# Soft-MoE tail of a fused attention kernel: last weight blocks loaded by column halves, first half combined and stored between

## The chip, the cores and the metric

One core of one Trainium2 chip runs the whole program. The metric is device microseconds of one execution. Before the change three runs gave a median of 540.23 us (538.64 to 541.44).

## The reference, cut to what matters

First an attention over 8 batches, 8 heads, 576 tokens and 64 dimensions: scores scaled by 1/8, everything more than `tau` under the row's maximum dropped, softmax, product with V. Its output, 4608 tokens by 512 columns, is the input `x` of a soft mixture of experts with 8 experts of 4 slots each:

```python
logits = x @ phi                                   # 4608 x 32
d = softmax over the tokens;  slot_input = d.T @ x # 32 x 512
for e in range(8):
    slot_out[e] = relu(slot_input[e] @ w1[e]) @ w2[e]   # w1 512x1024, w2 1024x512, 16.8 MB + 16.8 MB
c = softmax over the slots (of the same logits)
out = c @ slot_out                                 # 4608 x 512, 9.4 MB
```

All numbers are float32 in memory. Nothing of `out` can be written before `slot_out` is there, and each column of `slot_out` needs that column of all rows of all of `w2`.

## The kernel before

The attention takes the first 470 us or so. It is scheduled by a planner with a table of due times, and the change does not touch it. The program after it ("the tail") is in the order in which it is written.

**Weights.** `w1` and `w2` are cut into 64 blocks of 128 partitions by 1024 numbers (512 KB, 4 KB in each partition, which are 4 KB in a row in memory too). Blocks 1 to 32 are `w1`, 33 to 64 `w2`; a `w2` block holds 256 rows of one expert, two rows in each partition (`j`). `load_unit` (line 487) takes the next block and issues one DMA on SyncE's queue. 45 blocks are loaded during the attention; the other 19 are issued as the first product frees their places.

**Products.** Experts are worked on in two groups of four (`a`), each expert in its own 32 columns of TensorE's array, so that four matmuls run side by side. `stage1` (line 1051) multiplies by `w1`, `relu` and `hidden` make the transposed hidden layer `hz`, and `stage2` (line 1084) multiplies by `w2` in steps `k` of four blocks (one per expert). Of the last group, k = 0 and 1 end in the PSUM tile `so`; k = 2 goes by halves of 256 columns into two tiles `end[0]` and `end[1]`; k = 3 (the last four blocks) is spread over 128-column quarters, each in its own 32 columns of the array (lines 1088 to 1094).

**Slots.** `slots` (line 1123) adds the partial sums of the groups with a matmul by the constant `st4`, once on the part that is in `so` and once on the rest. ScalarE then writes `sh`, VectorE subtracts its own rounding from half the rows (lines 1135 and 1137), and `sh` (float32r) is ready in halves of columns.

**Output.** `combine` (line 1127) runs over 18 jobs of 256 tokens: 16 of 512 of a batch's 576 tokens (`b`, `k`), then two of the 64 left tokens of each batch. Each job is two matmuls of a transposed coefficient tile (`cTs[b]`) with `sh`, a copy by ScalarE, a copy by VectorE, and a DMA of 512 KB on SyncE's queue, 4 KB in a row per partition. The jobs of left rows are stored by two DMAs each, 64 partitions and 2 KB in a row. `ct` (line 1020) makes a coefficient tile: GpSimd multiplies, TensorE transposes (line 1045), ScalarE casts (line 1046), VectorE subtracts (line 1047); two are made early, the others one after each pair of jobs. The stores wait on SyncE's queue behind the loads and are issued in the order written.

Of the kernel before, what the change touches and what calls it, by code (L numbers as in the profile page):

```python
# [10 lines left out]
F32 = mybir.dt.float32  # L11
F32R = mybir.dt.float32r
AF = mybir.ActivationFunctionType
ALU = mybir.AluOpType
# [8 lines left out]
    k=2, q=2, vv=2, r=3, ri=1, nmx=4, thr=4, p2=4, pL=1, pTa=1, pTb=1, pla=1, plb=1, plL=1,  # L23
# [13 lines left out]
WARM = 17  # L37
FILL = 14
NHOST = 19
TABLE = {}  # L40
for _n, _v in (
    ("batch", [
# [321 lines left out]
def softmax_attention_soft_moe(  # L364
# [17 lines left out]
    nc = tc.nc  # L382
    B, HP, D, _, S = qT.shape
    NP = B * HP
    N9 = 9
    DM = out.shape[1]
    E, _, F = w1.shape
    NS = phi.shape[1]
    SPE = NS // E
    SM = 512  # L390
# [14 lines left out]
        out=st1, in_=ident.rearrange("p (g s) -> p s g", g=4), axis=AX.X, op=ALU.add  # L405
# [5 lines left out]
    def few(n):  # L411
# [12 lines left out]
        out=flag8, in0=tau_sb, scalar1=0.0, scalar2=0.125, op0=ALU.is_ge, op1=ALU.mult  # L424
# [22 lines left out]
    with tc.tile_pool(name="ps_up", bufs=1, space=PSUM) as up:  # L447
        t = up.tile([128, 512], F32, name="up")
# [5 lines left out]
        k=([128, S], F32), q=([128, 2, S], F32), vv=([128, 640], F32), p2=([128, 2 * S], F32), pL=([128, S + 3 * SL], F32),  # L454
        pTa=([128, 2, 4, QA], F32), pTb=([128, 2, 4, S - QA], F32), pla=([128, QA], F32), plb=([128, SM - QA], F32),
        ss=([128, S], F32), xT=([128, S], F32), x=([128, 4, DM], F32), xl=([128, DM], F32),
        d=([128, 384], F32), R=([128, S], F32), rt=([128, 128], F32),
# [17 lines left out]
    NG = E // 4  # L475
# [9 lines left out]
    where = {}  # L485

    def load_unit(t):

        if len(where) == len(units):
            return  # L490
        i, kind, _, e, k = units[len(where)]
        where[i] = t
        if kind == 0:
            nc.sync.dma_start(t, w1[e, k * 128:(k + 1) * 128, :])
        else:
            nc.sync.dma_start(t, w2[e, k * 256:(k + 1) * 256, :].rearrange("(p j) f -> p (j f)", j=2))


    rows = [slice(0, 64), slice(64, 128)]
# [497 lines left out]
    def ttile(name):  # L997
        return ps_t.tile([128, 512], F32, tag="t", name=name)
# [21 lines left out]
    def ct():  # L1020


        if len(cTs) == len(blocks):
            return
        while len(c4s) < min(len(cTs) + 2, len(blocks)):
            c4s.append(c_block(*blocks[len(c4s)]))
        k = blocks[len(cTs)][1]
        c4 = c4s[len(cTs)]
        n = 128 * k
        t = tx.tile([128, SM], F32R, tag="cT", name=f"cT{len(cTs)}", bufs=3)  # L1030
        if len(cTs) < 2:
            w = two(f"ct{len(cTs)}", "h00" if cTs else "h01")
            for i in range(k):
                split(w, i, c4[:, i].rearrange("p g s -> p (g s)"))
            tv = t.rearrange("p (i g q) -> p i g q", i=4, g=2)
            for g in range(2):
                wv = w[g][:, 0:256].rearrange("p (i q) -> p i q", i=4)
                nc.scalar.copy(tv[:, :, g], wv)
                nc.vector.tensor_tensor(
                    out=tv[64:128, :, g], in0=wv[64:128], in1=tv[64:128, :, g].bitcast(F32), op=ALU.subtract)  # L1040
            cTs.append(t)
            return
        w = ttile(f"ct{len(cTs)}")
        for i in range(k):
            tr(w[:, i * 128:(i + 1) * 128], c4[:, i].rearrange("p g s -> p (g s)"))
        nc.scalar.copy(t[:, 0:n], w[:, 0:n])
        nc.vector.tensor_tensor(  # L1047
            out=t[64:128, 0:n], in0=w[64:128, 0:n], in1=t[64:128, 0:n].bitcast(F32), op=ALU.subtract)
        cTs.append(t)
# [22 lines left out]
    def hidden(a, hid):  # L1072
        for n in range(2):
# [3 lines left out]
            for g, m in enumerate(rows):  # L1077
# [3 lines left out]
                    op=ALU.mult,  # L1081
                )

    def stage2(a, k):
        t = [where[n_units // 2 + a * 16 + k * 4 + g].rearrange("p (j f) -> p j f", j=2) for g in range(4)]

        if a == NG - 1 and k == 3:
            for g in range(4):
                for j in range(2):
                    for c in range(4):  # L1090
                        nc.tensor.matmul(
                            end[c // 2][c * 32:(c + 1) * 32, c % 2 * 128:(c % 2 + 1) * 128],
                            hz[:, a, k * 2 + j, g * 32:(g + 1) * 32], t[g][:, j, c * 128:(c + 1) * 128],
                            start=False, stop=(g == 3 and j == 1), tile_position=(0, 32 * c), skip_group_check=True)
            return
        apart = a == NG - 1 and k == 2
        for q, dst in enumerate(end if apart else [so]):
            c = slice(q * DM // 2, (q + 1) * DM // 2) if apart else slice(0, DM)
            for j in range(2):
                for g in range(4):  # L1100
                    nc.tensor.matmul(
                        dst[g * 32:(g + 1) * 32, 0:c.stop - c.start], hz[:, a, k * 2 + j, g * 32:(g + 1) * 32],
                        t[g][:, j, c], start=(j == 0 and (apart or a == 0 and k == 0)),
                        stop=(j == 1 and not apart and a == NG - 1 and k == 1),
                        tile_position=(0, 32 * g), skip_group_check=True)
        for g in range(4):
            load_unit(where[n_units // 2 + a * 16 + k * 4 + g])

# [2 lines left out]
    def otile(name):  # L1111
        cnt[0] += 1
        k = cnt[0] % 6
        return ps_h.tile([128, 512], F32, tag=("h01", "h10", "h11")[k // 2], name=name) if k % 2 else ttile(name)
# [6 lines left out]
        return [t for i, t in sorted(last.values(), key=lambda x: x[0])]  # L1121

    def slots(w, x, q, first):
        nc.tensor.matmul(w[:, 0:DM // 2], st4.rearrange("p g s -> p (g s)"), x[:, q * DM // 2:(q + 1) * DM // 2],
                         start=first, stop=not first)

    def combine():

        cols = [slice(n * DM // 2, (n + 1) * DM // 2) for n in range(2)]
        nc.scalar.copy(so_sb[:, 1, cols[0]], end[0][:, 0:DM // 2])  # L1130
        nc.vector.tensor_copy(so_sb[:, 1, cols[1]], end[1][:, 0:DM // 2])
        for q, x in enumerate(cols):
            w = sums[q]
            slots(w, so_sb[:, 1], q, False)
            nc.scalar.copy(sh[:, x], w[:, 0:DM // 2])
            nc.vector.scalar_tensor_tensor(
                out=sh[:, x], in0=sh[:, x].bitcast(F32), scalar=neg, in1=w[:, 0:DM // 2], op0=ALU.mult, op1=ALU.add)
        free = through()

        jobs = [(b, k) for b in range(B) for k in (0, 2)] + [(B, k) for k in range(0, B // 2, 2)]  # L1140
        ov = out.rearrange("(i h s) d -> h s i d", h=2, s=S)
        for n, (b, k) in enumerate(jobs):
            ot = free[n].rearrange("p (c d) -> p c d", c=2)
            token = lambda c: slice(k + c, SM, 4) if b < B else slice((k + c) * 128, (k + c + 1) * 128)
            ws = [otile(f"o{n}_{c}") for c in range(2 if n else 0)]
            for q, x in enumerate(cols if n == 0 else []):
                for c in range(2):
                    w = otile(f"o{n}_{c}_{q}")[:, 0:DM // 2]
                    nc.tensor.matmul(w, cTs[b][:, token(c)], sh[:, x], start=True, stop=True)  # L1149
                    if q:  # L1150
                        nc.vector.tensor_copy(ot[:, c, x], w)
                    else:
                        nc.scalar.copy(ot[:, c, x], w)
            for c in range(len(ws)):
                nc.tensor.matmul(ws[c], cTs[b][:, token(c)], sh, start=True, stop=True)
                if c == 0:
                    nc.scalar.copy(ot[:, c], ws[c])
                else:
                    nc.vector.tensor_copy(ot[:, c], ws[c])  # L1159
            if k:  # L1160
                ct()
            if b < B:
                nc.sync.dma_start(
                    out[b * S:b * S + SM].rearrange("(p c) d -> p c d", c=4)[:, k:k + 2], ot)
            else:
                for h in range(2):
                    nc.sync.dma_start(ov[h, SM:S, k:k + 2], ot[h * 64:(h + 1) * 64])

    hp = [[ps_h.tile([128, 512], F32, tag=f"h{a}{n}", name=f"h{a}_{n}") for n in range(2)] for a in range(NG)]
    hid = []  # L1170
    so = ps_h.tile([128, 512], F32, tag="so", name="so")
    end = [None, None]
    for a in range(NG):
        for kb in range(4):
            stage1(a, kb, hp[a])
# [11 lines left out]
        hid.append(relu(a, hp[a]))  # L1187
    ct()
    ct()
    end[:] = [ps_h.tile([128, 512], F32, tag=t, name=t + "e") for t in ("h00", "h11")]  # L1190
    for a in range(NG):
        for k in range(4):
            if a == NG - 1 and k == 2:
                so_sb = tx.tile([128, 2, DM], F32, name="so_sb")
                nc.scalar.copy(so_sb[:, 0], so)
            if a == NG - 1 and k == 3:
                sums = [ttile(f"sr{q}") for q in range(2)]
                for q, w in enumerate(sums):
                    slots(w, so_sb[:, 0], q, True)
            stage2(a, k)  # L1200
            if a < NG - 1 and k == 1:
                hidden(a + 1, hid[a + 1])
    combine()
    order_all.close()


# [45 lines left out]
```

## Time and profile before

| what | us |
|---|---|
| median of three runs | 540.23 |
| the profiled execution, its own time | 537.99 |
| its span, first to last instruction | 535.9 |
| first `w1` product of the tail starts | 472.9 |
| last weight block issued, landed | 493.9, 504.0 |
| first store issued | 508.7 |
| last copy of an output job ends | 525.3 |

Times below count from the start of the span. [...] On TensorE one float32 matmul leaves two records, one float32r matmul one.

### The profile page before, as it was taken

To read this page: it belongs to the slowest core of one execution; us is meant where nothing else is said; L and a number is where in the kernel's file an instruction comes from. 1 tells how busy PE (TensorE), PEld (TensorE's weight loads), DVE (VectorE), ACT (ScalarE), POOL (GpSimd) and SP (SyncE) were. 2 spreads that over 40 slices of the span, in tenths; PEclk is the share of its full clock that TensorE was granted. 3 is DMA by queue.
4 is the path that set the end of the run, shared out by engine and by line. 5 is a ranking of instruction groups with operands and counts; after the bars stand their busy time and mean duration, and the time that the engine had idled before them with its cause. 6 is when DMAs were issued, how large, how long until landed. Compare 5 with 4: busy or idle time off the path is not lost. (4 is left out here: it accounts for less than half of the span.)

```text
span 535.9 us, 18253 instructions
## 1 busy us (share of the span) xinstructions
PE 516.7 (96%) x6938; PEld 347.1 (65%) x6938; DVE 471.3 (88%) x1306; ACT 437.1 (82%) x785; POOL 243.4 (45%) x413
## 2 busy tenths in 40 slices
PE   8999999999999999999999999999999999999890
PEld 6666666676676676766766666766766766643560
DVE  6999999999999999999999999999999999713192
ACT  3898998988998899889988999889988999611280
POOL 1544564366534564455443643655345645121030
PEclk9999999999999999999999999999999999999996
DMA  6466686576557565444334444444344333999498
GB/s 160 96 192 192 196 192 185 169 213 201 144 154 197 184 182 154 121 115 101 107 93 115 115 115 116 115 116 114 98 125 113 99 90 111 394 406 408 186 392 314
DMA packets 37891, 92.32 MB, mean 172 GB/s; under 512 B 6068, under 2 KB 15020, under 8 KB 37804
## 3 DMA queue, kind: packets, MB, share of 16 engines
q1 hardware_dynamic: 37484, 90.90, 55.8%
q8 instruction: 55, 0.90, 0.7%
q10 hardware_dynamic: 320, 0.26, 0.2%
q14 instruction: 32, 0.26, 0.2%
HBM read 81.56 MB, written 9.58 MB: 170 GB/s over the span
## 5 line engine op out<-in xcount | busy, mean ns | idle before, releaser
L628 POOL TENSOR_SCALAR small<-small 128x1 f32<-128x1 f32 x288 | 143.6, 504 | 198.6 <-DVE ss L615 180.2
L615 DVE TENSOR_SCALAR_CACHE_REDUCE ss<-ps 128x576 f32<-128x576 f32 x288 | 209.0, 752 | 6.8 <-issue 2.0
L631 DVE SCALAR_TENSOR_TENSOR p<-ss,small,p 128x576 f32<-128x576 f32 x256 | 206.1, 825 | 0.9 <-POOL small L628 0.3
L625 ACT ACTIVATE p<-ss,small 128x576 f32<-128x576 f32 x256 | 186.4, 775 | 9.8 <-DVE ss L615 9.0
L603 PE MATMUL ps<-k,q 64*128 64x288 f32 x1024 | 159.1, 424 | 0.3 <-POOL k L567 0.2
L603 PEld LDWEIGHTS ps<-k,q 64*128 64x128 f32 x1024 | 85.5, 188 | 21.4 <-DVE ss L615 3.3
L514 PE MATMUL ps<-ident,p 64*128 64x64 f32 x2304 | 95.5, 224 | 0.6 <-ACT pTb L519 0.2
L514 PEld LDWEIGHTS ps<-ident,p 64*128 64x128 f32 x2304 | 86.2, 138 | 13.2 <-DVE ss L615 1.7
L519 ACT COPY pTb<-ps 128x1024 f32<-128x1024 f32 (+1 forms) x96 | 82.9, 875 | 10.8 <-PE ps L514 10.5
L724 PE MATMUL ps<-pTb,vv 128*64 128x320 f32 x512 | 76.0, 439 | 0.0
L519 ACT COPY pTa<-ps 128x1024 f32<-128x1024 f32 x64 | 63.2, 1012 | 0.8 <-PE ps L514 0.5
L724 PE MATMUL ps<-pTa,vv 128*64 128x256 f32 x512 | 62.3, 385 | 0.0
L724 PEld LDWEIGHTS ps<-pTb,vv 128*64 128x64 f32 x512 | 33.9, 136 | 34.0 <-ACT pTb L519 3.6
L735 POOL TENSOR_TENSOR xT<-xT,R 128x576 f32<-128x576 f32 x31 | 49.8, 1608 | 10.3 <-DMA R<-rd 5.7
L724 PEld LDWEIGHTS ps<-pTa,vv 128*64 128x64 f32 x512 | 33.9, 136 | 21.9 <-ACT pTa L519 3.6
L519 ACT COPY xT<-ps 128x256 f32<-128x256 f32 (+1 forms) x62 | 24.8, 399 | 5.5 <-PE ps L724 5.5
L631 DVE SCALAR_TENSOR_TENSOR pL<-ss,small,pL 128x576 f32<-128x576 f32 x32 | 28.2, 881 | 0.0
L625 ACT ACTIVATE pL<-ss,small 128x576 f32<-128x576 f32 x32 | 25.1, 786 | 3.1 <-DVE ss L615 3.1
L1012 POOL TENSOR_TENSOR c<-lall,crow 128x512 f32<-128x512 f32 x9 | 9.3, 1046 | 36.1 <-PE ct L506 22.4
L654 POOL TENSOR_SCALAR small<-small 128x9 f32<-128x9 f32 x31 | 16.6, 536 | 15.2 <-DVE p L631 8.1
L567 POOL TENSOR_SCALAR k<-k,small 128x576 f32<-128x576 f32 x31 | 23.5, 757 | 0.0
L615 DVE DVE_READ_ACCUMULATOR ss<-ps 128x1 f32 x288 | 23.4, 81 | 0.0
(163 smaller groups left out, 532.1 us busy)
## 6 DMA issues: line engine op xcount, KB each, us to landing
w<-in_w SPq DMA_DIRECT2D x45, 512.0 KB
q<-in_qT SPq DMA_DIRECT2D x62, 288.0 KB
vv<-in_vt SPq DMA_DIRECT2D x32, 320.0 KB
host<-in_w SPq DMA_DIRECT2D x19, 512.0 KB
k<-in_kT SPq DMA_DIRECT2D x62, 144.0 KB
R<-rd SPq DMA_DIRECT2D x62, 144.0 KB
out<-host SPq DMA_DIRECT2D x9, 512.0 KB
out<-w SPq DMA_DIRECT2D x7, 512.0 KB
```

The source lines that it names most:

```text
L514: nc.tensor.transpose(out=s[:, g, c:c + 64], in_=ins[g], identity=ident[rows[g], rows[g]], tile_position=(64 * g, 0))
L519: G.add("ACT", 51 + 0.833 * n, nom, lambda: nc.scalar.copy(*io()), r, w)
L567: scaled = lambda e, c=slice(0, S): lambda: e.tensor_scalar(out=kt.t[:, c], in0=kt.t[:, c], scalar1=flag8, **one)
L603: nc.tensor.matmul(s.t[:, g, 0:HS], qt.t[rows[g], h, c * 128:(c + 1) * 128], kt.t[rows[g], h * HS:(h + 1) * HS], start=True, stop=True, ti ...
L615: dve(674, t + OFF['mx'], [s], [ss, nmx], lambda s=s, ss=ss, nmx=nmx: nc.vector.tensor_scalar(out=ss.t.rearrange("p (a k) -> p a k", a=2), ...
L625: G.add("ACT", 668, t + OFF['ex'], lambda sv=sv, nmx=nmx, view=view: nc.scalar.activation(view().rearrange("p (a k) -> p a k", a=2), sv(), ...
L628: pool(250, t + OFF['th'], lambda nmx=nmx, thr=thr: nc.gpsimd.tensor_scalar(out=thr.t, in0=nmx.t, scalar1=1.0, scalar2=pabs, op0=ALU.mult, ...
L631: fn=lambda sv=sv, thr=thr, view=view, at=at: nc.vector.scalar_tensor_tensor(out=view().rearrange("p (a k) -> p a k", a=2), in0=sv(), scal ...
L654: pool(292, t + OFF['ri'], lambda: nc.gpsimd.tensor_scalar(out=ri.t[:, 0:N9], in0=r.t, scalar1=1e-9, scalar2=1.0, op0=ALU.add, op1=ALU.mul ...
L724: nc.tensor.matmul(W.t[h * 64:(h + 1) * 64, a, o:o + p0.shape[-1]], vv.t[:, v0:v0 + 64], p0, start=(kb == 0), stop=(kb == 4), tile_positio ...
L735: G.add("POOL", 1140, u + 5.6, own=own, r=[R], w=[xT], fn=lambda: nc.gpsimd.tensor_tensor(out=xT.t, in0=xT.t, in1=R.t, op=ALU.mult))
L1012: nc.gpsimd.tensor_tensor(out=c4, in0=lall[:, rows].unsqueeze(2).to_broadcast([128, k, 4, NS]), in1=crow[:, rows].unsqueeze(2).unsqueeze(3 ...
```

## The change

The last 8 of the 64 blocks are loaded by two DMAs each, one per half of the columns (1 KB pieces): the first halves of all eight in turn, and when the eighth has been issued, all eight second halves. `stage2` loses its special cases; `products` and `spread` do k = 2 and k = 3 of the last group, for one half of the columns. One `ct` moves ahead of them. `combine` finishes the first half of the columns, makes and stores the first half of jobs 0 to 5 (1536 tokens) by DMAs of 256 KB, with the second halves' products between them; then the second half of the columns follows for these jobs, and jobs 6 to 17 go as before. The four stores of left rows are issued last, on ScalarE's queue.

```diff
         if kind == 0:
             nc.sync.dma_start(t, w1[e, k * 128:(k + 1) * 128, :])
+        elif len(where) <= len(units) - HALVED:
+            nc.sync.dma_start(t, w2[e, k * 256:(k + 1) * 256, :].rearrange("(p j) f -> p (j f)", j=2))
         else:
-            nc.sync.dma_start(t, w2[e, k * 256:(k + 1) * 256, :].rearrange("(p j) f -> p (j f)", j=2))
+            halved.append((t.rearrange("p (j f) -> p j f", j=2), w2[e, k * 256:(k + 1) * 256, :].rearrange("(p j) f -> p j f", j=2)))
+            for q, x in enumerate(cols):
+                for t, w in halved[-1:] if q == 0 else halved if len(halved) == HALVED else ():
+                    nc.sync.dma_start(t[:, :, x], w[:, :, x])
...
+    def products(a, k, dst, x, first, last):
+        t = [where[n_units // 2 + a * 16 + k * 4 + g].rearrange("p (j f) -> p j f", j=2) for g in range(4)]
+        for j in range(2):
+            for g in range(4):
+                nc.tensor.matmul(
+                    dst[g * 32:(g + 1) * 32, 0:x.stop - x.start], hz[:, a, k * 2 + j, g * 32:(g + 1) * 32],
+                    t[g][:, j, x], start=(first and j == 0), stop=(last and j == 1),
+                    tile_position=(0, 32 * g), skip_group_check=True)
+
+    def spread(a, k, dst, x):
+        n = (x.stop - x.start) // 4
+        for g in range(4):
+            t = where[n_units // 2 + a * 16 + k * 4 + g].rearrange("p (j f) -> p j f", j=2)
+            for j in range(2):
+                for c in range(4):
+                    nc.tensor.matmul(
+                        dst[c * 32:(c + 1) * 32, c * n:(c + 1) * n], hz[:, a, k * 2 + j, g * 32:(g + 1) * 32],
+                        t[:, j, x.start + c * n:x.start + (c + 1) * n], start=False, stop=(g == 3 and j == 1),
+                        tile_position=(0, 32 * c), skip_group_check=True)
...
+        def half(n, q, eng=None):
+            b, k = jobs[n]
+            w = bank(f"o{n}_{q}")
+            ws = [w[:, 0:DM // 2], w[:, DM // 2:DM] if eng is not None else bank(f"o{n}_{q}b")[:, 0:DM // 2]]
+            for c in range(2):
+                nc.tensor.matmul(ws[c], cTs[b][:, slice(k + c, SM, 4)], sh[:, cols[q]], start=True, stop=True)
+            if eng is None:
+                for c in range(2):
+                    both[c](ots[n][:, c, cols[q]], ws[c])
+            else:
+                both[eng](ots[n][:, :, cols[q]], w.rearrange("p (c d) -> p c d", c=2))
+            nc.sync.dma_start(main(b, k)[:, :, cols[q]], ots[n][:, :, cols[q]])
...
+        nc.scalar.copy(so_sb[:, 1, cols[0]], end[0][:, 0:DM // 2])
+        summed(0)
+        slot_out(0)
+        half(0, 0)
+        half(1, 0, 0)
+        products(NG - 1, 2, end[1], cols[1], True, False)
+        half(2, 0, 1)
+        half(3, 0, 0)
+        products(NG - 1, 3, end[1], cols[1], False, True)
+        nc.vector.tensor_copy(so_sb[:, 1, cols[1]], end[1][:, 0:DM // 2])
+        half(4, 0, 0)
+        summed(1)
+        slot_out(1)
+        half(5, 0, 0)
+        half(0, 1)
+        for n in range(1, 6):
+            half(n, 1, n % 2)
+            if n % 2:
+                ct()
...
+        for n, (b, k) in enumerate(jobs):
+            if b == B:
                 for h in range(2):
-                    nc.sync.dma_start(ov[h, SM:S, k:k + 2], ot[h * 64:(h + 1) * 64])
+                    nc.scalar.dma_start(ov[h, SM:S, k:k + 2], ots[n][h * 64:(h + 1) * 64])
...
+        for k in range(4 if a < NG - 1 else 2):
             stage2(a, k)
             if a < NG - 1 and k == 1:
                 hidden(a + 1, hid[a + 1])
-    combine()
+    so_sb = tx.tile([128, 2, DM], F32, name="so_sb")
+    nc.scalar.copy(so_sb[:, 0], so)
+    ct()
+    end = [ps_h.tile([128, 512], F32, tag=t, name=t + "e") for t in ("h00", "h11")]
+    products(NG - 1, 2, end[0], cols[0], True, False)
+    sums = [ttile("sr0"), ps_h.tile([128, 512], F32, tag="so", name="sr1")]
+    for q, w in enumerate(sums):
+        slots(w, so_sb[:, 0], q, True)
+    spread(NG - 1, 3, end[0], cols[0])
+    combine(so_sb, end, sums)
```

## Rows read from the trace of the kernel before

**Rows 1.** Busy time by stretches: us, engines (instructions), granted clock, DMA share, GB/s.
```profile
core 0: us, PE busy (x) PEld busy (x) DVE busy (x) ACT busy (x) POOL busy (x), PEclk, DMA share, GB/s
500.00:502.00 2.00, 2.00 (x28) 1.20 (x20) 0.00 (x0) 0.25 (x1) 0.00 (x0) 1.00 0.79 313
502.00:504.00 2.00, 1.79 (x50) 1.25 (x48) 0.00 (x0) 0.00 (x0) 0.00 (x0) 1.00 0.15 59
504.00:506.00 2.00, 1.48 (x20) 1.05 (x20) 0.43 (x1) 0.47 (x2) 0.00 (x0) 1.00 0.00 0
506.00:508.00 2.00, 1.36 (x7) 1.10 (x5) 0.99 (x3) 1.19 (x4) 0.00 (x0) 1.00 0.00 0
508.00:510.00 2.00, 2.00 (x11) 1.81 (x10) 1.58 (x4) 1.52 (x4) 0.72 (x1) 1.00 0.22 90
```

**Rows 2.** The same view over the stores: main jobs, then left rows.
```profile
510.00:530.00 20.00, 12.42 (x53) 9.24 (x52) 14.87 (x23) 11.55 (x22) 4.52 (x5) 0.88 1.02 404
530.00:534.70 4.70, 0.00 (x0) 0.00 (x0) 0.00 (x0) 0.00 (x0) 0.00 (x0) 0.50 0.84 253
```

**Rows 3.** Chain of waits: start us, us, what.
```profile
493.93 10.09 DMA w<-in_w
```

**Rows 4.** Timeline of TensorE up to the last block: start, us, instruction, count, idle before.
```profile
499.37 1.05 PE L1101 MATMUL h00e<-w,hz 128*32 128x256 f32 x16
500.24 1.05 PE L1101 MATMUL h11e<-w,hz 128*32 128x256 f32 x16
501.21 1.13 PE L1124 MATMUL sr<-so_sb,st 128*128 128x256 f32 x4
502.27 0.30 PE L1091 MATMUL h00e<-w,hz 128*32 128x128 f32 x2
...
504.06 0.30 PE L1091 MATMUL h00e<-w,hz 128*32 128x128 f32 x2 [0.27 <-DMA w<-in_w]
```

**Rows 5.** Timeline of all engines from there to the first stores.
```profile
504.74 0.37 ACT L1130 COPY so_sb<-h00e 128x256 f32<-128x256 f32 x1 [4.49 <-PE h11e L1091]
...
505.17 1.13 PE L1124 MATMUL sr<-so_sb,st 128*128 128x256 f32 x4 [0.46 <-ACT so_sb L1130]
...
506.31 0.91 DVE L1136 SCALAR_TENSOR_TENSOR sh<-sh,neg,sr 128x256 fp32r<-128x256 f32 x2 [1.08 <-ACT sh L1135]
...
506.93 1.18 PE L1149 MATMUL o<-sh,cT 128*128 128x256 f32 x4 [0.64 <-DVE sh L1136]
...
507.95 0.74 PE L1155 MATMUL o<-sh,cT 128*128 128x512 f32 x2
...
508.53 0.60 PE L506 MATMUL ct<-ident,c 128*128 128x128 f32 x4
...
508.74 6.95 SPq L1163 DMA_DIRECT2D out<-w  x7
...
508.89 1.31 PE L1155 MATMUL o<-sh,cT 128*128 128x512 f32 x4
```

**Rows 6.** Groups of instructions, 498 to 528 us: busy us, mean ns, idle before.
```profile
L1159 DVE COPY host<-o 128x512 f32<-128x512 f32 x11 | 7.0, 685 | 0.1
L1157 ACT COPY host<-o 128x512 f32<-128x512 f32 x11 | 6.0, 590 | 1.0 <-PE o L1155 0.8
L1047 DVE TENSOR_TENSOR cT<-ct,cT 64x512 fp32r<-64x512 f32 x7 | 4.9, 695 | 0.6 <-ACT cT L1046 0.4
L1046 ACT CAST cT<-ct 128x512 fp32r<-128x512 f32 x7 | 4.1, 588 | 2.0 <-PE ct L506 1.9
```

**Rows 7.** One line's matmuls with 64 columns among them: ns min/median/max, first and last start.
```profile
L796 PE MATMUL ps<-xT,phi_sb x64: 219/246/297, 464.4 to 465.7; 128*32 128x128 f32 x32, 128*32 128x64 f32 x32
```

**Rows 8.** DMA queues, 474 to 484 us: packets, MB, share of 16 engines.
```profile
q1 hardware_dynamic: 1114, 4.06, 101.9%
```

**Rows 9.** DMA queues, 2 to 5 us: the queue whose packets are 1 KB.
```profile
q10 hardware_dynamic: 320, 0.26, 34.4%
```

**Rows 10.** Timeline of SyncE's queue: the stores of left rows.
```profile
527.19 5.00 SPq L1167 DMA_DIRECT2D out<-host  x4
```

**Rows 11.** Timeline: two engines on interleaved columns of one tile.
```profile
488.51 0.39 ACT L1038 CAST cT<-ct0b 128x256 fp32r<-128x256 f32 x1
...
488.66 0.43 DVE L1039 TENSOR_TENSOR cT<-ct0a,cT 64x256 fp32r<-64x256 f32 x1 [3.27 <-ACT cT L1038]
```

More of the change, by code (lines that the diff above doesn't have):

```diff
@@ L39 @@
 NHOST = 19
+HALVED = 8
 TABLE = {}
@@ L494, in load_unit @@
             nc.sync.dma_start(t, w1[e, k * 128:(k + 1) * 128, :])
-        else:
-            nc.sync.dma_start(t, w2[e, k * 256:(k + 1) * 256, :].rearrange("(p j) f -> p (j f)", j=2))
+        elif len(where) <= len(units) - HALVED:
+            nc.sync.dma_start(t, w2[e, k * 256:(k + 1) * 256, :].rearrange("(p j) f -> p (j f)", j=2))
+        else:
+            halved.append((t.rearrange("p (j f) -> p j f", j=2), w2[e, k * 256:(k + 1) * 256, :].rearrange("(p j) f -> p j f", j=2)))
+            for q, x in enumerate(cols):
+                for t, w in halved[-1:] if q == 0 else halved if len(halved) == HALVED else ():
+                    nc.sync.dma_start(t[:, :, x], w[:, :, x])
+    halved = []
+    cols = [slice(n * DM // 2, (n + 1) * DM // 2) for n in range(2)]
     rows = [slice(0, 64), slice(64, 128)]
@@ L1082, in hidden @@
                 )
-    def stage2(a, k):
[L1085 to L1105, printed above, removed]
@@ L1106, in stage2 @@
+    def stage2(a, k):
+        products(a, k, so, slice(0, DM), a == 0 and k == 0, a == NG - 1 and k == 1)
         for g in range(4):
@@ L1123, in slots, with combine @@
     def slots(w, x, q, first):
[L1124 to L1137, printed above, removed]
+        nc.tensor.matmul(w[:, 0:DM // 2], st4.rearrange("p g s -> p (g s)"), x[:, cols[q]], start=first, stop=not first)
+    def combine(so_sb, end, sums):
         free = through()
@@ L1141, in combine, with bank @@
         ov = out.rearrange("(i h s) d -> h s i d", h=2, s=S)
+        ots = [t.rearrange("p (c d) -> p c d", c=2) for t in free[:len(jobs)]]
+        main = lambda b, k: out[b * S:b * S + SM].rearrange("(p c) d -> p c d", c=4)[:, k:k + 2]
+        both = (nc.scalar.copy, nc.vector.tensor_copy)
+        turn = [0]
+        def bank(name):
+            turn[0] += 1
+            tag = ("h01", "h10", "", "h00")[(turn[0] - 1) % 4]
+            return ps_h.tile([128, 512], F32, tag=tag, name=name) if tag else ttile(name)
@@ new lines, in summed, with slot_out @@
+        def summed(q):
+            slots(sums[q], so_sb[:, 1], q, False)
+        def slot_out(q):
+            x, w = cols[q], sums[q][:, 0:DM // 2]
+            nc.scalar.copy(sh[:, x], w)
+            nc.vector.scalar_tensor_tensor(
+                out=sh[:, x], in0=sh[:, x].bitcast(F32), scalar=neg, in1=w, op0=ALU.mult, op1=ALU.add)
+        nc.scalar.copy(so_sb[:, 1, cols[0]], end[0][:, 0:DM // 2])
[4 more added lines that the diff above has]
+        products(NG - 1, 2, end[1], cols[1], True, False)
@@ L1142, in combine @@
+        half(2, 0, 1)
[11 more added lines that the diff above has]
+                ct()
         for n, (b, k) in enumerate(jobs):
-            ot = free[n].rearrange("p (c d) -> p c d", c=2)
+            if n < 6:
+                continue
+            ot = ots[n]
@@ L1144, in combine @@
             token = lambda c: slice(k + c, SM, 4) if b < B else slice((k + c) * 128, (k + c + 1) * 128)
[L1145 to L1153, printed above, removed]
@@ L1154, in combine @@
-            for c in range(len(ws)):
+            ws = [otile(f"o{n}_{c}") for c in range(2)]
+            for c in range(2):
                 nc.tensor.matmul(ws[c], cTs[b][:, token(c)], sh, start=True, stop=True)
[L1156 to L1159, printed above, removed]
+                both[c](ot[:, c], ws[c])
             if k:
@@ L1162, in combine @@
             if b < B:
-                nc.sync.dma_start(
-                    out[b * S:b * S + SM].rearrange("(p c) d -> p c d", c=4)[:, k:k + 2], ot)
-            else:
+                nc.sync.dma_start(main(b, k), ot)
+        for n, (b, k) in enumerate(jobs):
+            if b == B:
                 for h in range(2):
-                    nc.sync.dma_start(ov[h, SM:S, k:k + 2], ot[h * 64:(h + 1) * 64])
+                    nc.scalar.dma_start(ov[h, SM:S, k:k + 2], ots[n][h * 64:(h + 1) * 64])
     hp = [[ps_h.tile([128, 512], F32, tag=f"h{a}{n}", name=f"h{a}_{n}") for n in range(2)] for a in range(NG)]
@@ L1171, in softmax_attention_soft_moe @@
     so = ps_h.tile([128, 512], F32, tag="so", name="so")
-    end = [None, None]
     for a in range(NG):
@@ L1189, in softmax_attention_soft_moe @@
     ct()
-    end[:] = [ps_h.tile([128, 512], F32, tag=t, name=t + "e") for t in ("h00", "h11")]
     for a in range(NG):
[L1192 to L1199, printed above, removed]
+        for k in range(4 if a < NG - 1 else 2):
             stage2(a, k)
```

## The prediction

> **What bounds the kernel now.** I read the stretches of the tail first. The DMA engines move weights at about 408 GB/s until 500 us, then fall to 313, 59 and 0 GB/s, and come back in the stretch that begins at 508 [rows 1]. From 510 to 530 they are full again with stores at 404 GB/s [rows 2]. So the tail is a transfer that is cut in two. The hole: the loads' missing share is 0.42 + 1.70 us in 500 to 504, so their work ends on average at 501.9. The stores' 0.18 MB (90 GB/s in 2 us) take 0.44 us at full rate, so stores begin at 509.56. That is 7.7 us without data. After it, 16 main jobs at 512 KB / 404 GB/s = 1.30 us each end at 530.4, which is where the rate drops. The left rows (1.05 MB) then go at 253 GB/s and end at 534.7 [rows 2], and the span closes at 535.9.
>
> The chain of waits says that the last block issued at 493.93 ends the load at 504.02 [rows 3]. TensorE's timeline qualifies that: the engine is never idle before, and it waits only 0.27 us, for this one block, at 504.06 [rows 4]. So TensorE's own work reaches the last products hardly earlier than the data does. This decides the case: data that come earlier are of use only as far as TensorE is there to take them.
>
> From the last products the path to the first store is a chain of small steps [rows 5]: ScalarE's copy at 504.74, the slots' matmul 505.17, VectorE's step on `sh` 506.31, the first output matmul 506.93, four of them with four copies, the store issued at 508.74, data 0.82 us later.
>
> **The change part by part.**
>
> *Loads by halves.* A 4 KB packet costs 10 us x 16 x 1.019 / 991 packets = 164 ns [rows 8], which is 41 ns per KB. For 1 KB packets the trace has 256 of them at 3 us x 16 x 0.344 / 256 = 64 ns at most, at the start, when two queues run at once [rows 9]. So 41 to 64; I take 48, near the row of the same queue in the same steady stream. The slowest engine ends its share of the last eight blocks at about 503.9; 8 blocks of 8 packets at 164 ns are 10.5 us, so it begins them at 493.4. First halves: 8 x 16 x 48 ns = 6.1 us, landed by 499.5 (498.6 to 501.6). Second halves by 505.7 (503.9 to 509.8). The extra 1.8 us of loading lies in the hole.
>
> *TensorE up to the first half.* `so` ends and k = 2 begins at 499.37 as before. Then come the moved `ct` (0.36 us, from 508.53 to 508.89 [rows 5], and two changes of tile shape, 0.10 + 0.17 by the gaps at 501.21 and 502.27), one half of k = 2 in place of two (0.87, from 499.37 to 500.24), and the slots (0.10 + 1.06, from 501.21 to 502.27) [rows 4]. `spread` begins at 499.37 + 0.63 + 0.87 + 1.16 = 502.03, so it has its data and waits for none, unless 1 KB costs over 67 ns. Its 32 matmuls of 64 columns are 64 records. Groups of four with 128 columns take 0.11 us (the 128 records from 502.27 on, less the wait [rows 4]); a line with 32 records of each width spans 1.3 us [rows 7], so eight groups of the narrow kind took 1.3 - 8 x 0.11 = 0.44, or 0.055 each. 16 x 0.055 = 0.88 (upper end 16 x 0.11 = 1.76). ScalarE's copy then starts at about 503.15 instead of 504.74, **1.6 us sooner**, not the 4.4 us by which the data are earlier.
>
> *To the first store.* The same chain takes 506.93 - 504.74 = 2.19, so the first output matmul is at 505.34. With two matmuls instead of four (less 2 x 0.255, four take 506.93 to 507.95), the store goes out 1.81 - 0.51 = 1.30 later, at 506.64, and its data at 507.46: **2.1 us sooner** than 509.56.
>
> *The six early halves.* Each is 256 KB: 0.77 us of the DMA engines at 48 ns (0.65 to 1.02). On TensorE a half takes 0.51, a `products` 0.87 plus 0.30 of shape changes. In the written order the starts are 505.34, 505.85, products 506.36, 507.53, 508.04, products 508.55, 509.72. A store follows its half's start by 0.51 + 0.25, one copy of 0.59 (ScalarE) or 0.69 (VectorE) [rows 6] and 0.13. Stores: 506.6, 507.4, 509.1, 509.6, 511.2. Second columns: the second products end at 509.85, copy 0.43, slots and result at 511.06, ScalarE 0.4 behind the fifth half's copy, VectorE 511.5, and 0.6 later the first matmul on them at 512.1. The sixth store is at 512.2 (its copy queues behind ScalarE's step on `sh`), the seventh at 513.4. So up to 514.2 the DMA engines get 6 x 0.77 = 4.6 us of work in 6.7 us. **Compute feeds them too slowly here**, and 2.1 us of the hole come back as small holes.
>
> *The six second halves.* They bring three `ct`. VectorE has three copies, three subtractions and the next job's copy, 7 x 0.69 = 4.8 us, plus some 0.7 of waits for ScalarE's casts (0.59 each) [rows 6], from 513.4 to 518.9. Stores end at 517.5, and job 6, whole again, is issued at 519.0, its data at 519.8. Before, job 6 had its turn at 509.56 + 6 x 1.30 = 517.4. So the main stream is **2.4 us later**, although it began 2.1 us earlier. From there compute makes a job per 1.03 us against 1.30 of the DMA engines, as before, and ten jobs end at 519.8 + 13.0 = 532.8.
>
> *Left rows.* Before, 1.05 MB took 4.3 us behind everything, and the four issues held SyncE's queue 5.0 us [rows 10]. Afterwards ScalarE issues them after its last copy, near 528.5, beside main stores that run to 532.8. Bounds for what they add: 2.6 us at 404 GB/s, 4.3 as before. I take 3.0: the row of half-width stores is of stores alone, and these run beside full-width ones most of the time. The wait added to ScalarE (for VectorE's last copy) has nothing behind it.
>
> The half-rate of these stores is told by the row, 253 GB/s against 404. [...]
>
> *Edits that cost nothing:* the second group's `ct` casts (ScalarE and VectorE idle at 500 to 504 [rows 1]; without that cover 0.6 us), and the other bank order.
>
> **Sum.** 532.8 + 3.0 = 535.8 against 534.7: +1.1 us. On the profiled execution's 537.99 that is 539.1. The median shown is 2.24 above it, so 541.3 in its measure.
>
> **Rivals.**
>
> 1. *The hole is filled.* If the early chain is quicker (copies start before I think, TensorE's changes of shape cost less), the engines get data without a break from 507.46: 12 x 0.77 + 13.0 + 3.0 end at 532.7, and with 41 ns and 2.6 us 530.9. Gain 2.0 to 3.8, middle 2.9: 537.3. For it: ScalarE and VectorE are busy under half of 504 to 508 [rows 1]. Against it: the second columns' five-step chain lies between and cannot be shortened by idle engines.
> 2. *The second queue brings the left rows nothing.* They take their 4.3 us after or out of the main stores: +2.4, 542.6. [...] Against it: they no longer stand alone.
> 3. *The DMA engines' packets are dear.* At 64 ns the second halves land at 509.8, after TensorE asks for them at 508.75; from 60 ns on this decides, and all behind it slips by 1.0. With rival 2's price: +3.4, 543.6, slower than before. For it: the only 1 KB row. Against it: that row is from a start with two queues.
> 4. *The change doesn't do what it says:* the first products wait for both halves of a block, since both are in one tile. Then `spread` begins at 505.7, 3.7 later: 545.0. Against it: VectorE started on interleaved columns at 488.66 while ScalarE wrote the others until 488.90 [rows 11].
>
> **How the numbers follow.** Forecast 0.46 (its own range 539.0 to 542.6), rival 1 0.20, rival 2 0.16, rival 3 0.11, rival 4 0.07. A measurement of this kernel can tell about 0.5%, 2.7 us, from no change. Faster by more: two thirds of rival 1, 0.14. Slower: rivals 3 and 4 and a little of 2, 0.20. Same: 0.66. The range that leaves out 2 in 10 reaches from rival 1's middle to rival 3's time, 537.3 to 543.6.
>
> **What would show it.** First half's copy of `end[0]` near 503.2 and no DMA wait ahead of `spread` (rival 4: a wait there). First store near 506.6. DMA share about 0.7 between 507.5 and 514 (rival 1: above 0.95). First whole job's data near 519.8, the right figure to judge the sum by. DMA rate above 320 GB/s from 529 to the end (rival 2: a stretch at 250). A wait of TensorE on a load near 508.8 would be rival 3. The forecast is wrong if the stream of stores has no gap, or if the end of the last main job is not later than 530.4.

## The result and the profile after

The changed kernel takes 543.74 us in the median of 12 runs (540.33 to 547.32), the kernel before 540.19 on the same chip. The ratio is 1.0069, with a 95% interval of 1.0044 to 1.0094: the change makes the kernel slower by 3.7 us (2.4 to 5.1). The forecast was 541.3.

The profiled execution took 543.28 us with a span of 541.2, against 537.99 and 535.9. I measure the tail from the start of its first `w1` product to the end of the last data packet, because executions differ in what comes before it (that start lies between 472.7 and 476.6 us in the profiles of this document). The tail begins at 472.88 before and at 473.60 after, and takes 61.80 us before and 66.30 after: +4.5. "After the first product" below means after this start.

The first view is the busy time by stretches of the changed kernel, with the columns of [rows 1]: length, then TensorE, its weight loads, VectorE, ScalarE, GpSimd, granted clock, DMA share, GB/s.
```profile
494.00:500.00 6.00, 6.00 (x60) 1.68 (x52) 0.44 (x2) 0.00 (x0) 0.00 (x0) 1.00 1.07 340
500.00:502.00 2.00, 2.00 (x25) 1.14 (x22) 0.58 (x1) 1.10 (x2) 1.04 (x1) 1.00 1.05 338
502.00:504.00 2.00, 1.86 (x68) 1.32 (x66) 0.12 (x1) 0.07 (x1) 0.00 (x0) 1.00 1.02 329
504.00:506.00 2.00, 0.70 (x2) 0.30 (x2) 0.48 (x1) 0.67 (x2) 0.00 (x0) 1.00 0.29 97
506.00:508.00 2.00, 1.97 (x12) 1.41 (x16) 0.43 (x1) 0.96 (x2) 0.00 (x0) 0.71 0.00 1
508.00:510.00 2.00, 2.00 (x16) 1.07 (x8) 0.00 (x0) 0.00 (x0) 0.00 (x0) 0.50 0.78 262
510.00:512.00 2.00, 2.00 (x21) 1.13 (x20) 1.12 (x2) 0.59 (x1) 0.00 (x0) 0.93 0.19 60
512.00:514.00 2.00, 1.30 (x6) 1.10 (x6) 0.48 (x1) 1.53 (x3) 0.00 (x0) 1.00 0.77 263
514.00:516.00 2.00, 2.00 (x12) 2.00 (x12) 1.12 (x2) 0.98 (x3) 0.49 (x1) 1.00 0.66 219
516.00:518.00 2.00, 2.00 (x15) 2.00 (x14) 1.93 (x3) 1.54 (x3) 1.59 (x2) 1.00 1.06 347
518.00:520.00 2.00, 2.00 (x11) 1.58 (x10) 1.91 (x4) 1.57 (x3) 1.05 (x1) 1.00 0.49 162
520.00:522.00 2.00, 1.85 (x9) 1.56 (x10) 1.94 (x4) 1.64 (x4) 1.05 (x1) 1.00 1.05 371
522.00:531.80 9.80, 5.66 (x20) 3.94 (x19) 7.32 (x12) 5.23 (x10) 0.00 (x0) 0.95 1.02 403
531.80:539.90 8.10, 0.00 (x0) 0.00 (x0) 0.00 (x0) 0.00 (x0) 0.00 (x0) 0.50 0.85 264
```
Three things differ from [rows 1, 2]. The loads run on to about 504.6 at a share above 1 (340 and 338 GB/s: the same engines' time carries fewer bytes). Behind the hole, from 508 to 520, the stores have shares of 0.78, 0.19, 0.77, 0.66, 1.06 and 0.49, where the kernel before had full engines from 510 on. And the last stretch, from the first packet of the left rows, with all compute done, lasts 8.1 us at 264 GB/s, where it was 4.7 us at 253; it now has main stores among the left rows.

The timeline of the same stretch answers to [rows 5] and, in its last line, to [rows 10].
```profile
502.76 0.94 PEld L1108 LDWEIGHTS h00e<-w,hz 128*32 128x32 f32 x64 [0.33 <-DMA w<-in_w]
502.76 1.10 PE L1108 MATMUL h00e<-w,hz 128*32 128x64 f32 x64
503.93 0.37 ACT L1172 COPY so_sb<-h00e 128x256 f32<-128x256 f32 x1 [2.54 <-PE h00e L1108]
504.35 0.70 PE L1133 MATMUL sr<-so_sb,st 128*128 128x256 f32 x2 [0.49 <-ACT so_sb L1172]
505.49 0.48 DVE L1169 SCALAR_TENSOR_TENSOR sh<-sh,neg,sr 128x256 fp32r<-128x256 f32 x1 [3.38 <-ACT sh L1168]
506.03 0.51 PE L1155 MATMUL o<-sh,cT 128*128 128x256 f32 x1 [0.98 <-DVE sh L1169]
...
507.26 1.94 PE L1097 MATMUL h11e<-w,hz 128*32 128x256 f32 x16
507.30 12.66 SPq L1161 DMA_DIRECT2D out<-w  x12
...
510.35 1.07 PE L1097 MATMUL h11e<-w,hz 128*32 128x256 f32 x16
...
511.48 0.42 DVE L1181 COPY so_sb<-h11e 128x256 f32<-128x256 f32 x1 [0.79 <-PE h11e L1097]
...
513.73 0.48 PE L1155 MATMUL o<-sh,cT 128*128 128x256 f32 x1 [0.70 <-DVE sh L1169]
...
520.39 0.34 SPq L1203 DMA_DIRECT2D out<-w  x1
...
528.93 6.46 ACTq L1207 DMA_DIRECT2D out<-host  x4
```
The chain to the first half is there as drawn: `spread` at 502.76, ScalarE's copy 503.93, the first store issued at 507.30. The second half's first copy, at 511.48, comes 4.2 us after that store. Job 6, the first whole job, is issued at 520.39. The four stores of left rows hold ScalarE's queue for 6.46 us.

### The profile page after: what moved, and what is told of

The parts are those of the page before. It is cut to its first block, busy times and chain, and to the rows that moved or that the text cites. A ratio compares the mean times of both kernels' runs of the same rounds, so it can differ in the third digit from the quotient of the medians.

```text
span 541.2 us, 18318 instructions
## 1 busy us (share of the span) xinstructions
PE 520.1 (96%) x6964; PEld 348.3 (64%) x6964; DVE 471.7 (87%) x1305; ACT 437.6 (81%) x786; POOL 242.7 (45%) x413
## 5 line engine op out<-in xcount | busy, mean ns | idle before, releaser
L640 DVE SCALAR_TENSOR_TENSOR pL<-ss,small,pL 128x576 f32<-128x576 f32 x32 | 29.5, 922 | 0.0
```

Of the source, the lines that this page charges most:

```text
L640: fn=lambda sv=sv, thr=thr, view=view, at=at: nc.vector.scalar_tensor_tensor(out=view().rearrange("p (a k) -> p a k", a=2), in0=sv(), scal ...
```

## Experiments

The theory that I started from: the early half came as forecast, and the loss is in the last stretch, because the left rows' stores are slow in themselves and gain nothing from a second queue. Its rivals: a fall of TensorE's clock at 507 (0.50 in the view above, 1.00 up to 510 in the kernel before [rows 1]) that delays the second half; and the halved loads.

**Left rows back on SyncE's queue** (`left_on_sync`).
```diff
-                    nc.scalar.dma_start(ov[h, SM:S, k:k + 2], ots[n][h * 64:(h + 1) * 64])
+                    nc.sync.dma_start(ov[h, SM:S, k:k + 2], ots[n][h * 64:(h + 1) * 64])
```


> The changed kernel with one part undone: the four stores of left rows are issued last on SyncE's queue again. Theory A (the second queue costs time: in the changed kernel the last 2.26 MB took from 531.4 to 539.2 us, 289 GB/s, and the last of the closing waits come after the last landing): the left rows take 4.3 us after the main stores, the kernel is 1 to 2 us faster than the changed one, about 542. Theory B (the queue is indifferent, the loss is all in the supply of the early halves): within 0.5 us of the changed one. My forecast's own term (the second queue saves 1.3 us): 1 to 1.5 us slower than the changed one.

541.86 us, ratio 1.0042 (1.0025 to 1.0058); tail 64.03. Its last stretch, by busy time:
```profile
534.50:538.90 4.40, 0.00 (x0) 0.00 (x0) 0.00 (x0) 0.00 (x0) 0.00 (x0) 0.50 0.84 248
```
Its timeline at the second half:
```profile
508.54 1.07 PE L1097 MATMUL h11e<-w,hz 128*32 128x256 f32 x16
...
511.81 0.42 DVE L1181 COPY so_sb<-h11e 128x256 f32<-128x256 f32 x1 [0.81 <-PE h11e L1097]
```
The left rows take 4.4 us, as in the kernel before (its line stands at `left_rows_interleaved`). The second queue therefore saved nothing here. In this profile TensorE's clock stays at 1.00, the second half's products take 1.07 us instead of 1.94, and the copy of the second half comes 36.90 us after the first product instead of 37.88. So of the 2.3 us by which this tail is shorter, about 1.0 is the clock of one execution; the other 1.3 lie behind it. Between the medians the intervals overlap (1.0042 against 1.0069), so that the second queue costs time is seen in profiles alone.

**The kernel before with the left rows on ScalarE's queue** (`before_left_scalar`), the same part alone.
```diff
-                    nc.sync.dma_start(ov[h, SM:S, k:k + 2], ot[h * 64:(h + 1) * 64])
+                    nc.scalar.dma_start(ov[h, SM:S, k:k + 2], ot[h * 64:(h + 1) * 64])
```


> The kernel before with that one part alone: left rows issued on ScalarE's queue after its last copy, all else as before. Theory A: the stores of both queues share the engines at a rate near 290 GB/s, so nothing is won, and the kernel is 0.5 to 1.5 us slower than before. Theory B: no difference within 0.5 us. My forecast's term: 1.3 us faster than before.

539.30 us, ratio 0.9996 (0.9981 to 1.0011); tail 61.92 against 61.80. Its last stretch:
```profile
529.60:536.70 7.10, 0.00 (x0) 0.00 (x0) 0.00 (x0) 0.00 (x0) 0.00 (x0) 0.55 0.92 312
```
The longest of the waits of SyncE's queue from 520 to 538 us (line and releaser: us in total, times, longest):
```profile
SPq L1163 <- DMA out<-host: 5.8, 1, 5.8
```
The two queues (q10 is ScalarE's, with the left rows, q1 SyncE's, with main stores; packets, MB, share of 16 engines) from 530.6 to 533.6:
```profile
q10 hardware_dynamic: 444, 0.81, 87.8%
q1 hardware_dynamic: 8, 0.03, 2.3%
```
The 2.21 MB of this stretch are 1.05 of left rows and 1.16 of main stores. One after the other, at 253 and 404 GB/s [rows 2], they would take 4.2 + 2.9 = 7.1 us, and they take 7.1. But they did run nearly one after the other: SyncE waits 5.8 us for an earlier store's landing, so most of the left rows go while hardly a main store is there, and the main stores come last. This run shows that the second queue wins nothing in the kernel before. It doesn't show what happens when both kinds of stores are there at once; the changed kernel does.

**TensorE kept busy through the gaps** (`clock_filled`): the changed kernel with transposes that nobody reads.
```diff
+        warm = ps_h.tile([128, 512], F32, tag="h10", name="warm")
+
+        def idle(n):
+            for i in range(n):
+                tr(warm[:, i % 4 * 128:i % 4 * 128 + 128], ident)
...
+        idle(4)
         summed(0)
...
+        idle(9)
         half(0, 0)
```


> The changed kernel with 4 and 9 extra transposes of the identity on TensorE in the two gaps ahead of the first output half (0.4 and 0.9 us in which it waits anyway; their result is not used). Theory A: the granted clock, which fell to half from 506.9 to 510.3 in the changed kernel's profile after these gaps, stays at full speed; the second halves' products take 0.87 and not 1.9 us; the stream of stores starts as before but its second part comes 0.8 us earlier, so the kernel is 0.5 to 1 us faster than the changed one. Theory B (the fall comes from something else, or the stores have slack there): clock row unchanged, or time within 0.3 us.

542.87 us, ratio 1.0057 (1.0040 to 1.0074); tail 65.03. Its profile has no fall before 527.5. The median is lower than that of the changed kernel by less than the intervals tell apart.

**The filled gaps and the left rows on SyncE together** (`sync_and_filled`), the two edits above in one kernel.

> The changed kernel with two parts: left rows on SyncE's queue, and the extra transposes of clock_filled. Theory A (the clock's fall comes in some executions of left_on_sync too): 0.3 to 0.8 us faster than left_on_sync and less spread. Theory B (left_on_sync has no fall): the same within 0.3 us. Both: data end 64.0 us after the tail's first product, as in left_on_sync's profile without a fall.

541.83 us, ratio 1.0052 (1.0025 to 1.0078); tail 63.57. Its profile has no fall there either. Beside `left_on_sync` (1.0042) nothing is won. Both kernels with filled gaps, without the fall in their profiles, stay some 3 us above the kernel before (1.0057 and 1.0052), so the clock isn't the main part of the 3.7 us.

**The halved loads alone** (`halved_loads_alone`): the kernel before, its last eight blocks loaded as in the change, nothing else.
```diff
-        else:
+        elif len(where) <= len(units) - 8:
...
+            for q, x in enumerate(halfs):
+                for t, w in halved[-1:] if q == 0 else halved if len(halved) == 8 else ():
+                    nc.sync.dma_start(t[:, :, x], w[:, :, x])
...
```


> The kernel before with the last eight blocks loaded by halves of columns and nothing else changed: the products still need both halves. Theory A (1 KB packets cost 48 ns, so 1.8 us more loading, and TensorE waits for the last block): the last block lands 1.8 us later, near 505.8, and the kernel is 1.5 to 2 us slower than before. Theory B (the load's end has slack because TensorE is as late): under 0.5 us slower, since TensorE's wait of 0.5 us takes it up.

541.90 us, ratio 1.0044 (1.0026 to 1.0062); tail 64.14, +2.3. Its timeline:
```profile
502.47 3.21 PE L1108 MATMUL h11e<-w,hz 128*32 128x256 f32 x16 [0.57 <-DMA w<-in_w]
...
508.66 0.37 ACT L1137 COPY so_sb<-h00e 128x256 f32<-128x256 f32 x1 [6.93 <-PE h11e L1098]
...
512.66 3.47 SPq L1170 DMA_DIRECT2D out<-w  x4
```
The last load ends 32.39 us after the first product instead of 30.72, later by 1.67. This kernel's TensorE asks for the second halves of k = 2 at once, so it waits for them, and the copy of the result is 2.34 later (34.20 against 31.86). So the loads' end is about as late as foreseen, the kernel loses a little more than the 1.5 to 2 us expected, and the early half has to win that back.

**Other rows as left rows** (`left_rows_interleaved`): the kernel before, the last coefficients put in another order, so that a store of 64 tokens reads every second partition instead of 64 neighbouring ones. The bytes, the packets' size and the queue stay.
```diff
+        if len(cTs) == B:
+            tv = tv.rearrange("p (i s h) -> p i h s", i=k, h=2)
+            wv = wv.rearrange("p (i h s) -> p i h s", i=k, h=2)
...
-                    nc.sync.dma_start(ov[h, SM:S, k:k + 2], ot[h * 64:(h + 1) * 64])
+                    nc.sync.dma_start(ov[h, SM:S, k:k + 2], ot[h:128:2])
```


> The kernel before with one thing changed: the coefficients of the left rows are ordered so that a store of 64 rows reads every second partition of all 128 instead of 64 neighbouring ones; queue, sizes and packets (2 KB) stay. Theory A (the 250 GB/s of these stores comes from the half of the partitions that one store reads): the left rows go near 390 GB/s, 2.7 us instead of 4.4, and the kernel is 1.2 to 1.8 us faster than before. Theory B (it comes from 2 KB packets or from SyncE's issuing, about 1.2 us each): rate stays at 250, time within 0.5 us of before.

539.91 us, ratio 1.0012 (0.9992 to 1.0032); tail 61.00. The left rows from their first packet to the end of the data, first in the kernel before, then here:
```profile
530.30:534.70 4.40, 0.00 (x0) 0.00 (x0) 0.00 (x0) 0.00 (x0) 0.00 (x0) 0.50 0.83 246
```
```profile
533.40:537.40 4.00, 0.00 (x0) 0.00 (x0) 0.00 (x0) 0.00 (x0) 0.00 (x0) 0.50 0.72 272
```
The second of these stretches in two parts:
```profile
533.40:536.00 2.60, 0.00 (x0) 0.00 (x0) 0.00 (x0) 0.00 (x0) 0.00 (x0) 0.50 1.01 381
536.00:537.40 1.40, 0.00 (x0) 0.00 (x0) 0.00 (x0) 0.00 (x0) 0.00 (x0) 0.50 0.19 70
```
In time of all sixteen engines the same 1.09 MB cost 0.83 x 4.4 = 3.7 us before and 0.72 x 4.0 = 2.9 here. The price thus belongs to which partitions are read, not to these stores' size or queue. While the engines are full the rate is 381 GB/s here; before it would be 246 / 0.83 = 296, so part of the 253 of [rows 2] was engines without work. In this kernel the gain hardly reaches the time, against the 1.2 to 1.8 us expected: 1.4 us remain in which, at a share of 0.19, three of sixteen engines work on average.

**One early half** (`one_early_half`): left rows on SyncE, the second columns' products ahead of all jobs, only job 0 cut in two.
```diff
+        products(NG - 1, 2, end[1], cols[1], True, False)
...
-        half(0, 0)
-        half(1, 0, 0)
-        products(NG - 1, 2, end[1], cols[1], True, False)
-        half(2, 0, 1)
-        half(3, 0, 0)
...
+        half(0, 0)
...
-            if n < 6:
+            if n < 1:
```


> The changed kernel with left rows on SyncE's queue and only one early half: the second halves' products follow at once (k = 2 ahead of the first slots, k = 3 behind them), only half of job 0 is made early, and jobs 1 to 17 go whole. Theory A (the six early halves starve the DMA engines, since each delays the second columns' chain and is itself fed by one copy at a time): sh is complete about 4 us sooner than with six early halves, whole jobs stream from then on, and the kernel is 1 to 2 us faster than left_on_sync, near the kernel before. Theory B (the halved loads' 1.8 us are what is lost, wherever the stores start): as slow as left_on_sync and halved_loads_alone, 2.3 us over before.

540.56 us, ratio 1.0015 (0.9989 to 1.0040); tail 62.38.

**Three early halves** (`three_early_halves`): the same with the halves of jobs 0 to 2 early, the second products right behind the first slots.
```diff
-        half(0, 0)
-        half(1, 0, 0)
         products(NG - 1, 2, end[1], cols[1], True, False)
-        half(2, 0, 1)
-        half(3, 0, 0)
+        half(0, 0)
...
-            if n < 6:
+            if n < 3:
```


> Between one_early_half and left_on_sync: three early halves, with the second products right after the first slots. Theory A: time between the two, about 0.5 us over one_early_half. Theory B: the same as both.

539.93 us, ratio 1.0012 (0.9989 to 1.0035); tail 62.07. Its stretches behind the hole:
```profile
514.00:516.00 2.00, 2.00 (x13) 1.81 (x12) 1.56 (x3) 1.34 (x3) 1.04 (x1) 1.00 0.79 266
516.00:518.00 2.00, 1.94 (x11) 1.63 (x10) 1.89 (x3) 1.76 (x4) 1.04 (x1) 1.00 0.95 331
```
After these the shares stay at 0.94 or more, where the changed kernel's drop to 0.49 in 518 to 520. Against `left_on_sync` (tail 64.03), which has six halves and the same queue, three halves give 2.0 us back and one gives 1.6; the ratios agree (1.0012 and 1.0015 against 1.0042), though their intervals overlap. What stands between the first half and the second is thus a cost of its own; the halved loads' 2.3 us are then nearly paid (+0.3 and +0.6 over before). Both kernels also have the second columns' products earlier in the order than the changed one, and no run separates that from the number of halves.

**The changed kernel once more** (`changed_again`), unchanged, to see what belongs to one execution.

> The changed kernel once more, on one chip with the two below. Theory A (the clock's fall is a matter of the single execution): slower than before by 2.5 to 4 us in the median; whether its profile shows the fall from about 33 to 37 us after the tail's first product decides whether that fall belongs to the change or to the execution. Without it the data should end 65.0 us after the tail's first product, as in clock_filled, with it 66.3. Theory B (the fall comes with the change each time): the fall is there again.

542.21 us, ratio 1.0061 (1.0037 to 1.0084); tail 66.15. Its copies of the two halves, and its stretches:
```profile
504.66 0.37 ACT L1172 COPY so_sb<-h00e 128x256 f32<-128x256 f32 x1 [2.54 <-PE h00e L1108]
...
511.18 0.42 DVE L1181 COPY so_sb<-h11e 128x256 f32<-128x256 f32 x1 [0.81 <-PE h11e L1097]
```
```profile
506.00:508.00 2.00, 1.24 (x8) 1.11 (x12) 0.90 (x2) 0.57 (x2) 0.00 (x0) 1.00 0.05 15
508.00:510.00 2.00, 2.00 (x20) 1.33 (x20) 0.32 (x1) 0.59 (x1) 0.00 (x0) 1.00 0.52 175
531.30:539.80 8.50, 0.00 (x0) 0.00 (x0) 0.00 (x0) 0.00 (x0) 0.00 (x0) 0.50 0.81 247
```
The clock stays at 1.00 up to the end of the products in this execution, and the second half's copy comes 6.52 us after the first's, where it was 7.55 (503.93 to 511.48): the fall costs 1.03. The tail is only 0.15 shorter, because TensorE was 0.7 late here already at the first copy (31.05 us after the first product instead of 30.33) and the last stretch is 0.4 longer. The slow end is in both.

**The changed kernel with interleaved left rows** (`changed_interleaved`): the order of rows of `left_rows_interleaved`, the stores still on ScalarE's queue.
```diff
-                    nc.scalar.dma_start(ov[h, SM:S, k:k + 2], ots[n][h * 64:(h + 1) * 64])
+                    nc.scalar.dma_start(ov[h, SM:S, k:k + 2], ots[n][h:128:2])
```


> The changed kernel with the left rows' coefficients reordered so that each of their stores reads every second partition; they stay on ScalarE's queue. Theory A (on the second queue these stores cost 1 us more because half-partition reads slow the main stores beside them too): that extra is gone and the rate of the end rises from 290 to near 390 GB/s; the data end 1.5 to 2.5 us sooner, the kernel is about 2 us faster than changed_again. Theory B (the second queue costs by itself): less than 1 us faster.

540.91 us, ratio 1.0024 (1.0005 to 1.0043); tail 62.72, 3.4 shorter than in `changed_again`; 2.7 of it are the last stretch (5.8 us against 8.5), 0.7 the lateness named there. The DMA queues of the last stretch, first in the changed kernel (531.8 to 539.9), with the slices of that stretch above:
```profile
DMA  9999998989999999899799999999989964211000
q10 hardware_dynamic: 575, 1.05, 49.3%
q1 hardware_dynamic: 313, 1.09, 35.4%
```
then here (530.9 to 536.7):
```profile
DMA  8999999899999899999998999999999999899400
q10 hardware_dynamic: 575, 1.05, 48.1%
q1 hardware_dynamic: 313, 1.09, 48.0%
```
Each stretch is a sum of its shares times its length. Changed kernel: main 2.87 us, left rows 3.99, idle 1.24, together 8.1. Interleaved: 2.78, 2.79 and 0.22, together 5.8. The main stores cost nearly the same in both; from neighbouring partitions the left rows are dearer by 1.2 us and end raggedly, which costs another 1.0.

**Both remedies** (`three_interleaved`): `three_early_halves` with the left rows interleaved, on SyncE's queue.

> three_early_halves (left rows on SyncE's queue) with the same reordering of the left rows. From the two measured apart, 62.07 and 61.00 against 61.80 us from the tail's first product to the last data, the sum is 61.3: 0.3 to 0.8 us faster than before, which a median may not resolve. If the early halves' gain and the reordering hinder one another it is at or over before.

539.12 us, ratio 0.9991 (0.9968 to 1.0014); tail 61.72, where 61.3 was expected. It makes up what the change lost, but no gain over the kernel before can be told.

## Why the prediction was wrong

**The steps that held.** Times are after the first product, so that both executions can be compared.

| step | forecast | measured |
|---|---|---|
| 1 KB packet, ns | 48 (41 to 64) | 51.6 (340 GB/s in 494 to 500 are 1992 such packets, at a share of 1.07) |
| last load ends later by, us | 1.8 | 1.67 (loads alone) |
| wait for data ahead of `spread` | none | 0.33 us of one weight load, beside the slots' matmuls, as long as before |
| ScalarE's copy of the first half | 30.27 | 30.33 |
| first store issued | 33.76 | 33.70 |
| DMA share from first store's data to 514 | about 0.7 | 0.61 in the same 6.5 us; 0.73 in `left_on_sync` |
| job 6 issued | 46.1 | 46.8 |
| main stores end | 59.9 | 59.6 (`left_on_sync`) |

By these rival 1 (the hole is filled), rival 3 (dear packets) and rival 4 (the change doesn't do what it says) are out. The hole is still there: it is shorter, but the engines' share that is missing from 504.6 to 520 adds up to 7.5 us, since TensorE gets to the first half's result only 1.5 us sooner and the small stores leave gaps. One reading of the forecast is off without effect: the 128-column matmuls from 502.27 on [rows 4] leave 64 records, not 128; the 0.11 us for a group of four stands.

**The step that failed** is the last term, "I take 3.0: the row of half-width stores is of stores alone, and these run beside full-width ones most of the time". From the time at which main stores would have ended by themselves, the left rows cost 5.4 us: the last 8.1 us of the profile carry 2.14 MB, of which main's 1.09 MB take 2.7 us at 404 GB/s. No run shows 3.0 for left rows from neighbouring partitions: it was my estimate between the two bounds. `changed_again` shows the same end (247 GB/s), the sign that I had named for rival 2. That is rival 2's mechanism, and more than its price of 4.3, the upper of my two bounds. With 5.4 in place of 3.0 the sum is 1.1 + 2.4 = 3.5 us, against 3.7 measured in the medians; the interval of 2.4 to 5.1 wouldn't tell this from a sum 1 us away.

The cause is shown from both sides. Left rows read from every second partition, on the same queue beside the same main stores, cost 2.8 us of the engines, 3.0 with the idle rest, which is the forecast's figure; the ratio falls from 1.0061 to 1.0024, and the tail is then 0.9 us longer than before, where the forecast had 1.1. Left rows from neighbouring partitions are slow on SyncE alone too (248 GB/s). My reason, that they run beside full-width stores most of the time and so cost less, isn't borne out: packets from neighbouring partitions hold the sixteen engines for 3.99 us instead of 2.79, and main stores beside them cost their full 2.87 us on top.

The rates say the same: 246 to 253 GB/s over the whole stretch from 64 neighbouring partitions and 272 from every second one; while the engines are full 296 (an estimate, 246 / 0.83) and 381. And the second queue saved nothing in either kernel (0.9996 in `before_left_scalar`, 1.0069 with it against 1.0042 without it in the changed one).

**A smaller size.** The profiled execution lost 1.0 us more than 3.5, and that is the clock: the second half's copy came 37.88 after the first product, 36.90 in `left_on_sync`. This fall is not in every execution. Over 12 runs of the changed kernel the mean granted clock of the whole run is 0.987 or 0.988 in eight and 0.989 to 0.991 in four; the eight average 544.34 us and the four 542.76. (A fall of 3.4 us takes 0.003 off that mean, so the figure is a hint and no proof.) In `changed_again` four are at the lower figures, and both kinds average 542.7. Its price in the medians stays open, between nothing and 1.6 us.

**Where the gain went.** Halving the loads costs 2.3 us by itself. The first half then leaves early, and three early halves win back all but 0.3 of it. Six, with the second columns' products between them, lose 2 us again: the first five stand ahead of the second columns' result, and the six stores of 256 KB were issued over 6.75 us (507.30 to 514.05) with some 0.8 us of work for the engines in each. The left rows' second queue, meant by the forecast to take 1.3 us off the 4.3 at the end, took off none.

**What stays open:** how much the second queue costs by itself. In the kernel before it cost nothing (0.9996), but there the left rows ran nearly alone and full-width stores ended the stream. In the changed kernel the tails without the fall are 65.03 and 66.15 with it against 64.03 without it. Alone on SyncE's queue the left rows' stretch is 3.7 us of the engines and 0.7 idle (0.84 of 4.4 us); beside main stores they take 3.99, and 1.24 are idle. No run tells whether the mixing or the queue makes that difference. Open too are the clock's price and the parts of order and number in the early halves.

## What to carry to other kernels

A transfer that runs below full rate must be priced by what makes it slow. Here that was the partitions it reads: neither company (3.99 us of the engines beside main stores, 3.7 alone) nor another queue (0.9996 in `before_left_scalar`) sped it up, and another order of rows did (2.79 and 2.9). And work that is cut in two so that its first part can start early delays the second part by all that is put between them: cut as few pieces as bridge the gap.

## What was not expected of the hardware

- The same 1.05 MB of stores in 2 KB packets takes 3.99 us of the sixteen engines from 64 neighbouring partitions and 2.79 from every second one of 128, beside the same main stores. Alone, the stretch of such stores costs 3.7 and 2.9 us of the engines, at 246 and 272 GB/s over all of it.
- Full-width stores beside such stores are no gain: the engines' time of both adds up (2.87 and 3.99 us), the mixed stretch of the changed kernel goes at 264 and 247 GB/s in two executions, about what the narrow ones get alone (246 to 253), and with the rows interleaved the same bytes take 5.8 us instead of 8.1.
- Four issues of these stores hold ScalarE's queue 6.46 us, and SyncE's 5.00 [rows 10].
- TensorE's granted clock was 0.50 in 508 to 510 in one execution, after two idle gaps of 0.49 and 0.98 us, and 1.00 there in another of the same kernel with the same gaps (`changed_again`).
